# TensorE's order fixed by hand in an attention + FFN kernel: first batch by token chunk, q turned on TensorE, column-tiled v projection, q loads held back

## The chip, the cores and the metric

One core of a Trainium2 chip. The time is device microseconds of one execution, the median over several; a profiled execution gives the traces. The span in a profile runs from the first to the last instruction and is 1.7 to 3.5 us shorter than the time of the same execution. The kernel before took 481.86 us (481.56 to 485.2, three runs).

## The reference

```python
# q, k, v: 8 batches x 8 heads x 1024 tokens x 64; E, F: 64 x 1024
k_proj = einsum('ks,bhsd->bhkd', E, k)
v_proj = einsum('ks,bhsd->bhkd', F, v)
attn   = softmax(q @ k_proj.T / 8)                 # 1024 x 64 per head
x      = (attn @ v_proj), heads side by side       # 8192 x 512
h      = maximum(maximum(x @ w1, x @ w2), x @ w3)  # 8192 x 768
out    = h @ w_out                                 # 8192 x 512, fp32
```

## The kernel before

The matmuls take bf16; inputs are cast from fp32 by the load DMAs, issued from GpSimd (POOL). Each load of q, k or v brings one batch. For every batch VectorE copies q into a packed tile `q_p`, and a transpose DMA, issued from SyncE, turns it into `qT`, which the scores read.

```python
loads = ctx.enter_context(tc.tile_pool(name="loads", bufs=2))   # q_t, k_t, v_t: two of each
...
def attention(b, box):
    q_t, k_t, v_t = load(b)
    q_p = att.tile([P, NPAIR, SI, 2, D], BF16, name="q_p")
    for g in range(NPAIR):
        nc.vector.tensor_copy(out=q_p[:, g]..., in_=q_t[:, 2 * g:2 * g + 2, :, :])
    qT = att.tile([P, NPAIR * SI, P], BF16, name="qT")
    nc.sync.dma_start_transpose(out=qT, in_=q_p...)
    yield
    ...                                  # k projection (64 columns), transpose of it: kpT
    for si in range(SI):                 # v projection, fT twice side by side in lhsT
        nc.tensor.matmul(out=vp_ps, lhsT=fT2[:, si]..., rhs=v_t[:, :, si, :], ...)
    ...
    for g in range(NPAIR):               # 64x64 matmuls in groups of four (busy 0.41 us a group)
        ...                              # scores, exp
        yield
        ...                              # sums z and values av; 1/z as exp(-ln z); xT = av * zi
        yield

def ffn(b, xT):
    for ch in range(NCHUNK):             # two chunks of 512 tokens
        for jt in range(NJT):            # six steps: 12 matmuls of 128x512, then the maxout
            ...
            nc.scalar.copy(out=h1s, in_=h_ps[0])
            nc.vector.tensor_tensor(out=m12, in0=h_ps[1], in1=h1s, op=ALU.max)
            nc.vector.tensor_tensor(out=hT[:, jt, :], in0=h_ps[2], in1=m12, op=ALU.max)
            yield
        ...                              # 24 matmuls with w_out, copies, one 1 MB store
        yield
```

Attention of batch b+1 is interleaved with the FFN of batch b, one `yield` for one `yield`; the framework's scheduler then orders each engine's queue by its own estimate of when things are ready.

The softmax here doesn't subtract the row's maximum and nothing guards it: scores larger than these inputs give would overflow.

## Time and profile before

| stretch of the 475.6 us span | TensorE idle, us |
|---|---|
| 0 to 98 us | 66.6 |
| 98 to 470.3 us | 1.0 |
| 470.3 to 475.6 us (last copy and store) | 5.3 |

The idle times are stretch minus TensorE's busy time in this view of stretches (columns: stretch, its length, then busy time and count of TensorE, its weight loads, VectorE, ScalarE, POOL; granted TensorE clock, DMA share, which can read above 1, GB/s moved):

```profile
0.00:49.40 49.40, 3.69 (x34) 2.88 (x35) 4.04 (x11) 1.28 (x1) 12.02 (x20) 1.00 1.10 181
49.40:98.00 48.60, 27.71 (x146) 10.06 (x145) 15.34 (x25) 16.30 (x19) 4.38 (x5) 0.83 1.23 201
98.00:128.70 30.70, 30.66 (x161) 11.83 (x161) 16.43 (x26) 18.07 (x23) 1.76 (x2) 0.94 0.98 187
128.70:470.30 341.60, 340.68 (x1807) 144.38 (x1806) 152.18 (x217) 156.41 (x222) 7.88 (x9) 1.00 0.35 84
470.30:475.60 5.30, 0.00 (x0) 0.00 (x0) 0.00 (x0) 0.55 (x1) 0.00 (x0) 0.84 0.47 198
```

The chain of waits, in order of time (start, duration, what the end of the kernel hung on then):

```profile
14.28 35.10 DMA qT<-q_p
...
66.36 31.48 DMA qT<-q_p
97.88 0.64 PE ps_a L162 x4
...
128.74 4.35 PE ps_f L219 x19
...
144.66 1.73 PE ps_p L145 x8
...
177.90 4.35 PE ps_f L219 x19
...
470.27 0.59 ACT o_acc L226
```

Two transposes of 35.1 and 31.5 us hold up TensorE at the start. In the median a transpose takes 7.3 us from issue to landing, so these two share the DMA engines with something: the page's 40 slices show about 200 GB/s from 12 to 119 us, because loads run two batches ahead. From 98 us on TensorE is gapless, and one batch takes 177.90 - 128.74 = 49.2 us. Its v projection is eight matmuls a batch, 1.73 us in the chain; in the list of groups (busy us, mean ns of one; the first batch's eight, just after 28.9 us in which TensorE waited, took 3.54 us in the chain instead of 1.73):

```profile
L145 PE MATMUL ps_p<-v_t,fT_92 128*128 128x512 bf16 x64 | 16.8, 410 | 0.0
```

### The profile page before, as it was taken

Reading aid. Unit: us, or ns where it says so; the run is one execution under the profiler, and the core shown is the slowest. Engines: PE = TensorE matmul, PEld = TensorE weight load, DVE = VectorE, ACT = ScalarE, POOL = GpSimd, SP = SyncE. Lnnn points to the kernel's source line nnn. Section 1 sums busy time; section 2 is a strip of 40 time slices with the busy share of each in tenths; the row PEclk is TensorE's granted clock in tenths of the full one; section 3 lists DMA queues with packets and bytes.
Section 4 is the critical chain, followed back from the end, with each engine's and each line's share of the span. In section 5 each row is a group of like instructions: output and inputs, shape, how many; then the busy total and the mean of one; then the engine's idle time right before and its main releaser. Section 6 shows DMA issues by size and latency. Waiting matters only on the chain.

```text
span 475.6 us, 5314 instructions
## 1 busy us (share of the span) xinstructions
PE 402.7 (85%) x2144; PEld 169.1 (36%) x2144; DVE 188.0 (40%) x277; ACT 192.6 (41%) x265; POOL 26.0 (5%) x36
## 2 busy tenths in 40 slices
PE   0200679079999999999999999999999999999995
PEld 0100124023344434443443344434443444334442
DVE  0300156035633463435443634363435453454251
ACT  1000562036524653366236641664266415652322
POOL 7110002000010000000010001000000000000000
PEclk9999979779999999999999999999999999999999
DMA  7999999999589232944276236614101020202012
GB/s 120 202 201 196 206 206 196 196 208 216 109 176 170 97 90 88 144 123 90 88 110 156 64 114 94 150 35 121 45 10 79 0 90 0 91 0 88 34 55 88
DMA packets 62839, 54.06 MB, mean 114 GB/s; under 512 B 33760, under 2 KB 60640, under 8 KB 60768
## 3 DMA queue, kind: packets, MB, share of 16 engines
q0 software_dynamic: 27488, 28.58, 37.7%
q1 hardware_dynamic: 35328, 25.17, 18.2%
q8 instruction: 16, 0.26, 0.2%
q14 instruction: 7, 0.06, 0.0%
HBM read 57.15 MB, written 16.78 MB: 155 GB/s over the span
## 4 chain that ended last, share of the span: by engine, by line
PE 73%; DMA 18%; ACT 5%; issue 2%; DVE 1%; POOL 0%; POOLq 0%; DVEq 0%
PE ps_f L202 47%; PE ps_f L219 16%; DMA qT<-q_p 16%; PE ps_a L178 3%; PE ps_p L145 3%; PE ps_a L162 2%; DMA k_t<-in_k_dram 2%; ACT zl L185 2%; ACT zi L187 2%; PE ps_p L122 1%; ACT pT L169 1%; POOL q_t L99 0%; DVE hT L213 0%; DVE m_2011 L212 0%; DVE m_3352 L212 0%
## 5 line engine op out<-in xcount | busy, mean ns | idle before, releaser
L202 PE MATMUL ps_f<-xT,w_sb 128*128 128x512 bf16 x1152 | 265.7, 382 | 1.8 <-DVE xT L188 1.8
L202 PEld LDWEIGHTS <-w_sb 128*128 128x128 bf16 x1152 | 107.9, 98 | 142.0 <-issue 23.1
L219 PE MATMUL ps_f<-wout_sb,hT 128*128 128x512 bf16 x384 | 87.7, 379 | 0.9 <-DVE hT L213 0.3
L210 ACT COPY h1s<-ps_f 128x512 f32<-128x512 f32 x96 | 55.9, 583 | 75.8 <-PE ps_f L202 75.8
L188 DVE TENSOR_TENSOR xT<-ps_a,zi 128x1024 bf16<-128x1024 f32 x32 | 39.2, 1225 | 92.0 <-ACT zi L187 92.0
L169 ACT ACTIVATE pT<-ps_a 128x1024 bf16<-128x1024 f32 x32 | 32.8, 1024 | 83.5 <-PE ps_a L162 83.5
L226 ACT COPY o_acc<-ps_f 128x512 f32<-128x512 f32 x64 | 37.1, 584 | 50.7 <-PE ps_f L219 50.4
L219 PEld LDWEIGHTS <-hT 128*128 128x128 bf16 x384 | 36.3, 98 | 50.2 <-issue 5.4
L162 PE MATMUL ps_a<-qT,kpT 64*64 64x512 bf16 x128 | 14.0, 428 | 44.5 <-DMA qT<-q_p 43.9
L185 ACT ACTIVATE zl<-ps_a 128x1024 f32<-128x1024 f32 x32 | 32.8, 1024 | 44.0 <-PE ps_a L178 44.0
L187 ACT ACTIVATE zi<-zl 128x1024 f32<-128x1024 f32 x32 | 33.8, 1057 | 1.0
L162 PEld LDWEIGHTS <-kpT 64*64 64x64 bf16 x128 | 4.0, 105 | 58.4 <-issue 57.8
L109 DVE COPY q_p<-q_t 128x1024 bf16<-128x1024 bf16 x32 | 12.5, 442 | 28.5 <-DMA qT<-q_p 17.0
L145 PE MATMUL ps_p<-v_t,fT_92 128*128 128x512 bf16 x64 | 16.8, 410 | 0.0
L178 PE MATMUL ps_a<-pT,ones 64*64 64x512 bf16 x128 | 13.7, 417 | 3.3 <-ACT pT L169 3.3
L99 POOL DMA_DIRECT2D k_t<-in_k_dram x8 | 7.1, 894 | 144.3 <-PE ps_p L122 137.4
L152 ACT CAST vp<-ps_p 128x512 bf16<-128x512 f32 x8 | 4.7, 586 | 22.6 <-PE ps_p L145 22.6
L178 PE MATMUL ps_a<-pT,vp 64*64 64x512 bf16 x128 | 13.0, 392 | 0.1
L122 PE MATMUL ps_p<-k_t,eT_91 128*64 128x256 bf16 x128 | 9.9, 294 | 2.0 <-DMA k_t<-in_k_dram 2.0
L99 POOL DMA_DIRECT2D q_t<-in_q_dram x8 | 7.1, 888 | 65.1 <-DVE q_p L109 49.0
L99 POOL DMA_DIRECT2D v_t<-in_v_dram x8 | 7.0, 878 | 59.0 <-PE ps_p L145 54.8
L178 PEld LDWEIGHTS <-ones 64*64 64x64 bf16 x128 | 4.0, 105 | 17.2 <-issue 14.2
(219 smaller groups left out, 170.4 us busy)
## 6 DMA issues: line engine op xcount, KB each, us to landing
out_dram<-o_acc SPq DMA_DIRECT2D x16, 1024.0 KB, 3.8
q_t<-in_q_dram POOLq DMA_DIRECT2D x8, 1024.0 KB, 14.7
k_t<-in_k_dram POOLq DMA_DIRECT2D x8, 1024.0 KB, 12.5
v_t<-in_v_dram POOLq DMA_DIRECT2D x8, 1024.0 KB, 13.3
w_sb<-in_moe_w_dram POOLq DMA_DIRECT2D x3, 768.0 KB, 27.4
wout_sb<-in_moe_w_out_dram POOLq DMA_DIRECT2D x1, 768.0 KB, 35.2
e_sb<-in_E_dram POOLq DMA_DIRECT2D x1, 128.0 KB, 3.0
f_sb<-in_F_dram POOLq DMA_DIRECT2D x1, 128.0 KB, 3.0
```

The lines of the kernel that those rows point to most:

```text
L99: nc.gpsimd.dma_start(out=t, in_=src.rearrange("h (p si) d -> p h si d", si=SI))
L145: nc.tensor.matmul(out=vp_ps, lhsT=fT2[:, si].rearrange("p x k -> p (x k)"), rhs=v_t[:, :, si, :], start=(si == 0), stop=(si == SI - 1),)
L162: nc.tensor.matmul(out=sc[c * HALF:(c + 1) * HALF, hp, :], lhsT=kpT[rows, g % 2, g // 2, :], rhs=qT[rows, g * SI + 4 * c:g * SI + 4 * c + ...
L169: nc.scalar.activation(out=pT, in_=sc, func=AF.Exp, scale=scale)
L178: nc.tensor.matmul(out=dst[hp * HALF:(hp + 1) * HALF, c, :], lhsT=ones[rows] if w is None else w[rows, 2 * g + hp, :], rhs=pT[rows, hp, :] ...
L185: nc.scalar.activation(out=zl, in_=z, func=AF.Ln)
L187: nc.scalar.activation(out=zi, in_=zl, func=AF.Exp, scale=-1.0)
L188: nc.vector.tensor_tensor(out=xT[:, g].rearrange("a (c si) p -> a c (si p)", c=2), in0=av, in1=zi, op=ALU.mult,)
L202: nc.tensor.matmul(out=h_ps[i], lhsT=w_sb[i][:, ct, jt * P:(jt + 1) * P], rhs=rhs_x[:, ct, :, :], start=(ct == 0), stop=(ct == NCT - 1),)
L210: nc.scalar.copy(out=h1s, in_=h_ps[0])
L219: nc.tensor.matmul(out=o_ps, lhsT=hT[:, jt, tt * P:(tt + 1) * P], rhs=wout_sb[:, jt, :], start=(jt == 0), stop=(jt == NJT - 1),)
L226: nc.scalar.copy(out=o_acc[:, tt, :], in_=o_ps)
```

## The change

The intent: no transpose DMA in the first batch, an earlier first FFN matmul, a shorter attention on TensorE, and no transposes starved by loads. All PSUM tiles come from one pool of eight, TensorE's order is the program's order, and attention work hangs on fixed FFN steps. Core of the diff (cut, and the plan and the stores in shorthand; the softmax and FFN arithmetic is the same in halves):

```diff
-    loads = ctx.enter_context(tc.tile_pool(name="loads", bufs=2))
+    loads = ctx.enter_context(tc.tile_pool(name="loads", bufs=1))
+    psum = ctx.enter_context(tc.tile_pool(name="psum", bufs=8, space=bass.MemoryType.PSUM))
+    ctx.enter_context(tc.manual_schedule(engines={mybir.EngineType.PE}))
...
+    nc.gpsimd.dma_start(out=k_t, in_=view(k, 0))                       # k first
+    nc.gpsimd.dma_start(out=q_t[:, :, 0:SPC], in_=view(q, 0)[:, :, 0:SPC])   # then half of q
...
+    load_w(0, 1)                                                       # weights in slices
...
     def load(b):
+        dma = nc.gpsimd.dma_start(out=q_t, in_=view(q, b))
+        if b - 1 in last_T:                     # q of b waits for the transpose of b-1
+            tc.add_manual_dep(dma.ins, last_T[b - 1].ins.name, ... Sync ...)
+        nc.gpsimd.dma_start(out=k_t, in_=view(k, b))
+        nc.gpsimd.dma_start(out=v_t, in_=view(v, b))
+    def q_by_dma(b):                            # VectorE copies, then the transpose DMA
...
+    def q_by_pe(b, g, c):                       # batch 0 only: 8 transposes on TensorE
...
     for si in range(SI):                        # v projection
-        nc.tensor.matmul(out=vp_ps, lhsT=fT2[:, si]..., rhs=v_t[:, :, si, :], ...)
+        for hh in range(2):
+            nc.tensor.matmul(out=ps[hh * HALF:(hh + 1) * HALF, 0:4 * D], lhsT=fT[:, si, :],
+                             rhs=qkv[b][2][:, 4 * hh:4 * hh + 4, si, :], ...)
...
+    plan, batch 0:   (0, 2): [sc(0, 0, c1), sc(0, 1, c1), qd(1)], ...   # qd = q_by_dma
+                     (1, 1): [kv(1)], (1, 2): [kt(1), sc(1, 0), ld(2)], ...
+    plan, later b:   (0, 0): [qd(n)], (0, 2): [kv(n)], (0, 3): [kt(n), ld(n + 1)],
+                     (0, 4): [sc(n, 0)], (0, 5): [zav(n, 0), sc(n, 1)], ...      # n = b+1
+    stores of 256 tokens, the last ones of 128, instead of 512
```

## The prediction

> **What bounds the kernel now.** From about 128 us on TensorE is gapless: in the chain of waits a batch takes 49.2 us (128.74 to 177.90), of which 192 FFN matmuls at 0.216 us are 41.4 and attention 7.8. Before that DMA bounds it: in the 40 slices the queues move about 200 GB/s from 12 to 119 us (loads run ahead), and the q transpose, 7.3 us alone, shares with them and takes 35.1 and 31.5 us. In the chain these two stand before the scores; the second stall ends at 98 us. After the last FFN matmul (470.3 us) come 5.3 us of copy and 1 MB store.
>
> **What the change does.**
> 1. Batch 0: q is turned on TensorE by token chunk, without transpose DMA. k lands at about 12 us (now the first 1 MB lands at 12.5); projection and 32 cold transposes reach 18 us; then ScalarE paces (16 activations at 0.58 us, vp copies, multiplies). FFN starts at about 31 us instead of 69.
> 2. v projection column-tiled: 1.72 us becomes 0.99 (what k takes). Five groups of 64x64 matmuls instead of eight, about 0.1 us each. Batch period 48.1: 7 us in all.
> 3. Last stores per 128 tokens: tail 3.5 us.
> 4. q loads wait for the previous transpose, so transposes run at about 7.3 us.
>
> **What it costs.** The changed kernel's instruction order shows VectorE with q copies in its queue where q is not there yet. Loads come as k1, v1, q1, then q2 (after transpose 1), q3 (after transpose 2). VectorE blocks, PSUM isn't freed, TensorE stops:
> - Copies of q1 stand before the maxout of step 3 of batch 0's first chunk (about 45 us). About 9.6 MB come first; at 200 GB/s[...], q1 lands at about 55. Stall 10 us.
> - q2 lands 17 us after q1 (copies 1.9, transpose 7.3, load 8): stall 1 to 2.
> - q3 lands 17 us after q2; its first copy stands ahead of a maxout and the kT copy in step 2 of batch 0's second chunk, which the scores need: stall 12 us.
> - After each long stall TensorE restarts cold (granted clock 0.50 at 90 to 100 us now[...]): 2 us each.
> - Batch 0's second chunk: ScalarE 4.1 us per step against TensorE 3.7: 2 us.
> Later q loads are late too, but the slack of the down steps covers them.
>
> **Sum.** q1 at 55; scores of batch 1 resume 36 later (91); rest of batch 0 18; seven FFN batches and six attentions 330; cold starts, small stalls and tail 8: span 447. Runs now read 3 to 6 us above the span: 451 us, 8 in 10 between 437 and 466. Faster by over 2%: 0.93; within 2%: 0.055; slower: 0.015.
>
> **What would show it.** FFN start near 31 us; VectorE waits of about 10 us on q loads (L141) two or three times before 100 us, then little; TensorE gapless from there at a period of 48; transposes near 7 us; v projection 1.0.
>
> **What would make it wrong.** Faster loads (q1 at 48) or VectorE waits hidden by PSUM slack: 437 or less. q late in every batch, [...]: 460 and more.

What is cut: an allowance for the loads of weight slices, a second ground for the cold restarts, and two risks among those for 460 and more. The sum came to 447 us of span, 451 of time, and is left as it was, though the allowance is cut: 9.6 MB at 200 GB/s are 48 us, and the allowance is part of what was added up to q1's landing at 55. What the traces show for three other terms: "cold" is 4.33 us for 12 FFN matmuls after the second stall (98.52 us in the chain before) against 2.70 later; 0.1 us for a group of 64x64 matmuls is an estimate from the timeline before, where a group of four took 0.34 us until the next matmul (198.07 to 198.41) and one of eight 0.56 (201.10 to 201.66), 0.12 more than 0.22 for every four; 8 us for a load is assumption; in the kernel before the fastest load of k took 9.4 us from issue to landing, that of q 9.8.

## The result, and the profile after

461.56 us (458.25 to 463.42, four runs) against 481.71 (479.01 to 485.2, four runs); ratio 0.957, 95% interval 0.949 to 0.965. Ratios here are the mean time of one kernel's fast runs over that of the other's of the same rounds, so not quite the ratio of the medians.

The same view of stretches, now of the changed kernel (span 460.0 us):

```profile
0.00:28.20 28.20, 15.37 (x106) 8.42 (x106) 5.64 (x13) 10.08 (x19) 15.30 (x25) 1.00 1.24 173
28.20:48.00 19.80, 19.11 (x106) 7.43 (x105) 7.37 (x14) 7.86 (x14) 1.95 (x3) 1.00 1.31 204
48.00:56.00 8.00, 0.00 (x0) 0.00 (x0) 1.99 (x5) 0.12 (x1) 0.00 (x0) 0.69 0.79 132
56.00:79.00 23.00, 21.98 (x116) 9.49 (x115) 9.95 (x19) 8.32 (x15) 0.87 (x1) 0.89 0.68 134
79.00:94.00 15.00, 0.53 (x6) 0.25 (x6) 3.34 (x9) 0.95 (x2) 2.63 (x3) 0.59 0.99 180
94.00:136.00 42.00, 38.52 (x230) 16.31 (x226) 20.69 (x37) 21.26 (x42) 2.62 (x3) 0.94 0.89 163
136.00:338.70 202.70, 193.62 (x1101) 87.83 (x1098) 95.33 (x157) 97.17 (x185) 9.62 (x11) 0.97 0.56 117
338.70:455.90 117.20, 117.13 (x619) 51.92 (x618) 52.92 (x80) 54.09 (x102) 0.00 (x0) 1.00 0.16 56
455.90:460.00 4.10, 0.00 (x0) 0.00 (x0) 0.00 (x0) 0.56 (x1) 0.00 (x0) 1.00 0.35 130
```

| TensorE idle, us | before | after |
|---|---|---|
| start (before: to 98 us; after: to 136 us) | 66.6 | 40.5 |
| middle | 1.0 | 9.2 |
| tail | 5.3 | 4.1 |

The start has 26 us less idle time, and 8 us were given back in a stretch that had been gapless: 136 to 338.7 us holds 9.1 us without TensorE work. Its busy total rose by 3.5 us (402.7 to 406.3). 19.2 less idle and 3.5 more busy make, but for rounding, the 15.6 us by which the span fell.

Where the idle time went, in the chain of waits after:

```profile
38.05 15.94 DMA q_t<-in_q_dram
...
55.47 7.29 DMA qT<-q_p
63.32 11.39 DMA q_t<-in_q_dram
...
82.92 9.54 DMA q_t<-in_q_dram
...
107.64 5.52 DMA qT<-q_p
113.71 10.90 DMA q_t<-in_q_dram
...
153.47 5.51 DMA qT<-q_p
159.54 12.94 DMA q_t<-in_q_dram
...
338.70 5.29 PE bank L305 x24
...
375.89 0.87 PE bank L198 x16
...
385.97 5.29 PE bank L305 x24
...
455.87 0.58 ACT o_sb L312
```

The long transposes are gone (5.5 to 7.3 us each), and in their place stand loads of q, one after the other with the transposes: the rule of the diff shows as transpose, then load, then copies, then the next transpose. From batch 1 on that next transpose also waits for a free `qT` (there are two): the copies of batch 4's q were through at 127.3 us, but its transpose starts at 153.47, when the last scores of batch 2 (153.02 us) have read theirs. After the last q (275 us) batches take 385.97 - 338.70 = 47.27 us; before that they take up to 53.9 us (steps between the w_out groups that start at 136.11, 185.73, 237.58 and 291.43 us are 49.6, 51.9 and 53.9). By the list of waits VectorE stands 74.6 us, seven times, at most 12.8 us, before q copies (columns: who waits for whom; us in total, times, longest):

```profile
DVE q_p L141 <- DMA q_t<-in_q_dram: 74.6, 7, 12.8
```

How a late q stops TensorE is seen in the timeline (start, us, engine, line, instruction, and in brackets the idle time before it and what ended it):

```profile
54.01 1.43 DVE L141 COPY q_p<-q_t 128x1024 bf16<-128x1024 bf16 x4 [12.83 <-DMA q_t<-in_q_dram]
55.36 0.68 DVE L294 TENSOR_TENSOR m_436<-bank,h1s 128x512 f32<-128x512 f32 x1
...
56.09 0.64 PE L242 MATMUL bank<-pT,vp 64*64 64x512 bf16 x2 [8.61 <-DVE m_436 L294]
...
92.48 0.43 DVE L141 COPY q_p<-q_t 128x1024 bf16<-128x1024 bf16 x1 [11.02 <-DMA q_t<-in_q_dram]
...
93.42 0.28 DVE L190 COPY kpT<-bank 128x256 bf16<-128x256 bf16 x1
...
93.76 0.64 PE L225 MATMUL bank<-qT,kpT 64*64 64x512 bf16 x4 [14.14 <-DVE kpT L190]
...
172.50 1.43 DVE L141 COPY q_p<-q_t 128x1024 bf16<-128x1024 bf16 x4 [10.49 <-DMA q_t<-in_q_dram]
...
174.59 1.06 PE L172 MATMUL bank<-k_t,eT 128*64 128x256 bf16 x16 [2.29 <-DVE m_1421 L294]
```

The maxout m_436 had its data at about 44 us. It stood in VectorE's queue behind the q copies: it starts when the copies are through, at 55.36 us. Until then its bank isn't free and TensorE waits 8.6 us. The same thing happens at 92.5 us with the small copy of the k projection, which the scores need: 14.1 us. The copies stand there because VectorE's order is still the scheduler's (e4 shows that freeing TensorE's order too changes nothing in this): it moved VectorE's copies of q up to two batches earlier than the program has them. Batch 5's, for one, ran at 172.5 us in the first FFN step of batch 2 (last two lines); the program has them after the first step of batch 4. Presumably it took q to be ready there; no run shows what it assumed.

### The profile page after: what moved, and what is told of

Same layout as the page of the kernel before. It is cut to its first block, busy times and chain, and to the rows that moved or that the text cites. A ratio compares the mean times of both kernels' runs of the same rounds, so it can differ in the third digit from the quotient of the medians.

```text
span 460.0 us, 5849 instructions
## 1 busy us (share of the span) xinstructions
PE 406.3 (88%) x2272; PEld 181.7 (39%) x2272; DVE 197.2 (43%) x328; ACT 200.4 (44%) x377; POOL 33.0 (7%) x45
## 4 chain that ended last, share of the span: by engine, by line
PE 60%; DMA 29%; issue 4%; DVE 3%; ACT 2%; POOL 0%; POOLq 0%; DVEq 0%
PE bank L284 39%; DMA q_t<-in_q_dram 19%; PE bank L305 13%; DMA qT<-q_p 8%; PE bank L242 3%; DMA k_t<-in_k_dram 2%; PE bank L172 2%; PE bank L198 2%; PE bank L225 2%; DVE q_p L141 1%; ACT pT L235 1%; DVE hT L295 0%; ACT zl L256 0%; PE bank L156 0%; ACT zi L258 0%
## 5 line engine op out<-in xcount | busy, mean ns | idle before, releaser
L284 PE MATMUL bank<-xT,w_sb 128*128 128x512 bf16 x1152 | 266.1, 387 | 2.7 <-DVE m_950 L294 1.8
L292 ACT COPY h1s<-bank 128x512 f32<-128x512 f32 x96 | 56.4, 589 | 102.6 <-PE bank L284 82.1
L305 PE MATMUL bank<-wout_sb,hT 128*128 128x512 bf16 x384 | 85.8, 380 | 0.0
L235 ACT ACTIVATE pT<-bank 128x512 bf16<-128x512 f32 (+1 forms) x72 | 39.2, 598 | 48.3 <-PE bank L225 48.2
L268 DVE TENSOR_TENSOR xT<-bank,zi 128x512 bf16<-128x512 f32 x64 | 41.3, 686 | 36.3 <-ACT zi L258 35.9
L256 ACT ACTIVATE zl<-bank 128x512 f32<-128x512 f32 x64 | 35.1, 597 | 42.7 <-PE bank L242 42.1
L312 ACT COPY o_sb<-bank 128x512 f32<-128x512 f32 x64 | 36.9, 593 | 27.9 <-PE bank L305 27.9
L141 DVE COPY q_p<-q_t 128x1024 bf16<-128x1024 bf16 x28 | 10.3, 422 | 74.6 <-DMA q_t<-in_q_dram 74.6
L258 ACT ACTIVATE zi<-zl 128x512 f32<-128x512 f32 x64 | 37.1, 632 | 0.0
L225 PE MATMUL bank<-qT,kpT 64*64 64x512 bf16 x128 | 16.3, 409 | 14.6 <-DVE kpT L190 14.4
L211 ACT CAST vp<-bank 64x256 bf16<-64x256 f32 x16 | 5.8, 364 | 33.8 <-PE bank L198 19.5
L242 PE MATMUL bank<-pT,ones 64*64 64x512 bf16 x128 | 17.6, 411 | 1.8 <-ACT pT L235 1.8
L213 DVE CAST vp<-bank 64x256 bf16<-64x256 f32 x16 | 6.8, 427 | 14.1 <-ACT vp L211 13.9
## 6 DMA issues: line engine op xcount, KB each, us to landing
v_t<-in_v_dram POOLq DMA_DIRECT2D x7, 1024.0 KB, 13.5
q_t<-in_q_dram POOLq DMA_DIRECT2D x7, 1024.0 KB, 12.9
```

The costliest lines, as they stand in the source:

```text
L141: nc.vector.tensor_copy(out=q_p[:, g].rearrange("p si h d -> p h si d"), in_=qkv[b][0][:, 2 * g:2 * g + 2],)
L225: nc.tensor.matmul(out=sc[hp][c * HALF:(c + 1) * HALF, :], lhsT=kpTs[b][rows, g % 2, g // 2, :], rhs=qTs[b][rows, lo:lo + SPC, :], start=T ...
L235: nc.scalar.activation(out=pTs[b, g][r, hp, :], in_=sc[hp][r], func=AF.Exp, scale=scale)
L242: nc.tensor.matmul(out=dst[hp * HALF:(hp + 1) * HALF, :], lhsT=w(rows, hp), rhs=pTs[b, g][rows, hp, :], start=True, stop=True,)
L256: nc.scalar.activation(out=zl, in_=z[c], func=AF.Ln)
L258: nc.scalar.activation(out=zi, in_=zl, func=AF.Exp, scale=-1.0)
```

## The experiments

All kernels gave a correct result. Times are medians of four runs; each group of four experiments ran on a chip of its own, none of them beside the changed kernel, so small differences between groups should not be read. The record calls a run slow when it is over 1.5% above the fastest of its kernel. The kernel before, run beside them, scattered more than the others: 478.1 to 491.2 us in the first four experiments' rounds, 478.2 to 490.2 in the next four's (where six of seven runs lay above 486), 479.7 to 493.7 in the last four's. The comparisons with it are therefore marked unclear where a verdict was given, though most effects below are far larger than that scatter; smaller ones are read from the profiles.

My theory after reading the trace: what the change still loses is VectorE standing in order before q loads that come late; not DMA bandwidth, and not TensorE's own work. Rivals: the loads themselves are the limit; or the hand order on TensorE is what paid.

### e1_copies_held: the copies of batches 2 to 7 stay at their program place

```diff
+            cp = nc.vector.tensor_copy(out=q_p[:, g]..., in_=qkv[b][0]...)
+            if b >= 2:      # an order on VectorE's queue only: after the last maxout issued so far
+                tc.add_manual_dep(cp.ins, last_max[0].ins.name, ... NoSync, SCHED_ONLY ...)
```

> The changed kernel with one edit: VectorE's q copies of batches 2 to 7 are kept at their place in the program (after the first FFN step of the batch before), instead of one batch earlier where the scheduler put them. My theory: what the change still loses after 77 us is VectorE standing in order before q loads. From the trace: the stall of 79 to 94 us and its cold restart (18.5 us by comparison with an undisturbed second chunk), 3.8 us in batch 1, and 2.3, 4.6 and 6.6 us in batches 2 to 4, in all 36 us; so 424 to 428 us, VectorE waits for q only before batch 1's copies (about 13 us), every batch from 1 on at 47.3 us. Rival: the DMA queues are the limit and the wait only moves to the transposes and scores: 450 us or more, TensorE waiting on qT.

Measured: 428.21 us (427.25 to 429.13), span 426.8. The timeline shows the copies 47.27 us apart, with no wait before them but the first:

```profile
54.38 1.43 DVE L142 COPY q_p<-q_t 128x1024 bf16<-128x1024 bf16 x4 [13.89 <-DMA q_t<-in_q_dram]
100.77 1.42 DVE L142 COPY q_p<-q_t 128x1024 bf16<-128x1024 bf16 x4
148.04 1.42 DVE L142 COPY q_p<-q_t 128x1024 bf16<-128x1024 bf16 x4
```

The theory holds, in size too: 33 us against 36 expected (428.2 is just outside the range). The waits did not move to transposes (5.5 to 7.3 us) or scores.

### e2_q1_late: batch 1's copies later as well

```diff
-                (0, 2): [sc(0, 0, c1), sc(0, 1, c1), qd(1)],
+                (0, 2): [sc(0, 0, c1), sc(0, 1, c1)],
...
-                (0, 5): [zav(0, 2, c1), zav(0, 3, c1)],
+                (0, 5): [zav(0, 2, c1), zav(0, 3, c1), qd(1)],
```

> As the run before, and the copies of batch 1's q too are moved, from step 2 to step 5 of batch 0's first chunk. My theory: the stall of 48 to 56 us and its cold restart (about 2 us) go as well, the transpose still lands (about 63 us) before the scores of batch 1 are due (about 68): 413 to 418 us. Rival: the loads themselves bound the first 60 us (q1 can't be had sooner), the stall turns into a wait of batch 1's scores for qT or k: 424 or more.

Measured: 415.85 us (414.78 to 417.48), ratio to before 0.865 (interval 0.858 to 0.872). TensorE has almost nothing left to wait for from 30 us on (stretches as above):

```profile
0.00:30.00 30.00, 15.47 (x108) 8.50 (x109) 6.58 (x15) 10.09 (x19) 15.90 (x26) 0.88 1.24 174
30.00:90.00 60.00, 58.53 (x351) 25.34 (x350) 32.02 (x56) 34.26 (x64) 3.98 (x5) 0.97 1.00 185
90.00:410.00 320.00, 320.00 (x1814) 143.19 (x1813) 159.64 (x259) 155.79 (x293) 13.13 (x15) 1.00 0.52 114
```

q1 still landed at about 55 us; VectorE waited 3.3 us for it, and TensorE no longer at all. Loads were not the limit. This version beats both kernels.

### e3_no_throttle: the changed kernel without the rule on q loads

```diff
-        if b - 1 in last_T:
+        if False:
```

> The changed kernel without the rule that a q load waits for the transpose of the batch before (the single q buffer stays, so it waits for the copies). My theory: each q comes 7 us sooner, a transpose now shares with one load and takes 8 to 14 us; the VectorE waits shrink but stay: 445 to 456 us. Rival: the rule is what keeps transposes alive, without it they take 30 us as in the kernel before: 470 or more.

Measured: 449.88 us (449.11 to 451.1), 12 us faster than with the rule (0.937 of before, against 0.957). VectorE's wait on q loads fell from 74.6 to 22.6 us (plus 12.3 on earlier transposes), and transposes took up to 16.4 us instead of 7.3. In the changed kernel as it stands, the rule costs more than it gives.

### e4_pe_free: TensorE's order left to the scheduler

```diff
-    ctx.enter_context(tc.manual_schedule(engines={mybir.EngineType.PE}))
```

> The changed kernel with TensorE's order left to the scheduler too. My theory: the order by hand is worth little, since TensorE was gapless before from 128 us on and the gain came from the start and from smaller tiles: 455 to 468 us. Rival: the hand order is what pays: 475 or more.

Measured: 466.15 us (464.65 to 468.52), 1% above the changed kernel (not run side by side). The VectorE waits on q are the same (77.9 us, seven times). The hand order on TensorE alone is worth little here, where VectorE's waits set the time; with the copies late (e2) it was not tested.

### e5_before_pe_turn: only TensorE transposes in batch 0, in the kernel before

```diff
+        if b == 0:      # 64 small transposes through PSUM, VectorE copies
+            ...
+        else:
             ...         # q_p and the transpose DMA as before
```

> The kernel before, with one part of the change: batch 0's q is turned on TensorE (64 small transposes) instead of by a transpose DMA. My theory: the first stall (to 49 us) goes and batch 0's FFN starts near 35 us, but the transpose of batch 1 still shares the queues with loads that run ahead and takes 20 to 30 us, so only part of the first stall is gained: 456 to 470 us. Rival: the start is all there is to gain and this alone equals the whole change or better: 455 or less, no long transpose left.

Measured: 472.94 us (472.37 to 474.15); the kernel before beside it 478.2 to 490.2. Just outside my range. The mechanism held, and more came with it: the transpose of batch 1 was issued at 45 us among the loads and took 32.0 us to land (TensorE waited 7.1 us for it), that of batch 2 took 41.0 us; VectorE's next q copies waited 15.8 us for the latter, a maxout stood behind them, and TensorE waited 10.7 us. Turning q on TensorE removed one stall and left the others.

### e6_before_throttle and e7_before_both: the rule in the kernel before, alone and with e5

```diff
+            if nm == "q_t" and b - 1 in last_T:      # e6; e7 has e5's edit too
+                tc.add_manual_dep(dma.ins, last_T[b - 1].ins.name, ... Sync ...)
```

> The kernel before, with another part alone: a q load waits for the transpose of the batch before. My theory: the transpose of batch 0 still takes about 30 us (its own loads and the weights are ahead of it), that of batch 1 falls from 31 us to 15 or less, and VectorE now waits for late q loads as in the changed kernel: 455 to 472 us. Rival: no gain, the time is lost again in the q loads: 476 or more.

> Both parts in the kernel before (no hand order, no smaller tiles, no token chunks in the start). My theory: they carry most of the change's gain at the start; batch period still 49.2 us; VectorE waits for q loads: 443 to 462 us. Rival: they overlap and give no more than one alone: 463 or more.

Measured: 514.17 us (512.2 to 516.22) and 493.24 us (492.09 to 495.71). Both expectations were wrong: the rule makes the kernel before slower, by 36 us against the one fast run beside it (478.18), and still by 15 us with e5's part; the rivals' times were right. The list of waits of e6 has the changed kernel's trouble, and more of it:

```profile
DVE q_p L118 <- DMA q_t<-in_q_dram: 83.8, 7, 20.6
```

The first transpose still took 30.1 us to land, and only then was q of batch 1 loaded.

### e8_before_v_tiled: only the column-tiled v projection

```diff
+            for half in range(2):
                 nc.tensor.matmul(
-                out=vp_ps, lhsT=fT2[:, si]..., rhs=v_t[:, :, si, :],
+                    out=vp_ps[half * HALF:(half + 1) * HALF, 0:4 * D], lhsT=fT2[:, si, half, :],
+                    rhs=v_t[:, 4 * half:4 * half + 4, si, :],
```

> The kernel before, with the column-tiled v projection alone. My theory: 0.8 us per batch on a gapless TensorE, 5 to 7 us in all: 472 to 478 us, v projection 1.0 us per batch. Rival: [...] the four small copies eat the gain: 480 or more.

(Cut: a second supposed cause in the rival.)

Measured: 474.6 us (473.92 to 475.38). Against the scattered runs of the kernel before that says little, but the k loads, one a batch, come 48.5 and 48.6 us apart (188.99, 237.52, 286.14 us) instead of 49.6 and 49.3 (188.73, 238.30, 287.56): 0.6 to 1.0 us a batch, and the v projection takes 1.0 us (194.01 to 195.01), as expected.

### e9_late_no_throttle: e2 without the rule

> The version with all q copies late (e2), without the rule that a q load waits for the previous transpose. Theory now: the rule itself is no gain; it made q late, and lateness hurt only because VectorE stood before it. With the copies late there is slack: a transpose may share with one load (8 to 14 us instead of 6) and nothing waits: 413 to 419 us, as e2. Rival: transposes need the rule: 424 or more, scores waiting on qT.

Measured: 464.87 us (463.59 to 467.12), 49 us slower than e2. My theory (rule useless, lateness the only trouble) fell. The list of waits:

```profile
PE bank L233 <- DMA qT<-q_p: 36.5, 6, 8.3
```

Without the rule the load of the next q starts in the same moment in which the copies free the single q buffer, which is when the transpose starts (trace: transpose at 155.29, load at 155.53 us; behind it in the queue follow k at 159.64 and v at 160.51). The transposes then took 15.8 us in the median instead of 5.7. With the copies at their program place a transpose has about 10 us until the scores want it (in e2 184.72 to 194.97 us: FFN steps and the projections). 16 is too long: TensorE waits 6 us in each of six batches and restarts slowly (12 matmuls in 4.2 us instead of 2.7).

### e10_before_hold and e11_before_hold_throttle: held copies in the kernel before, without and with the rule

> The kernel before with one edit: VectorE's q copies of batches 1 to 7 are kept at their program place, after the first FFN step of the batch before; no rule on loads. Theory: the transpose of batch 1 starts near 72 us when most run-ahead loads are done, takes 15 us or less instead of 31, and the second stall shrinks from about 16 us to 5 or less; the first (to 49 us) stays; batch period 49.2: 462 to 474 us. Rival: the loads keep the queues full to 119 us whatever the copies do, the transpose still takes 25 us or more: 478 or more.

> The kernel before with the held copies and the rule that a q load waits for the previous transpose (which alone made it 514 us). Theory: the rule costs only through VectorE standing before a late q, so with held copies it costs nothing: as the run before within 1.5%, no VectorE wait on q loads after batch 1. Rival: the rule costs by itself, q or the transposes come too late in every batch: 490 or more.

Measured: 490.7 us (488.83 to 497.3), ratio 1.022; and 465.07 us (464.63 to 465.84), ratio 0.964. Held copies alone do not help, and e10 missed its range. Batch 1's transpose did shrink as expected (15.2 us, TensorE waited 5.2 us), but the next three took 15.7 to 16.0 us as well, which the expectation had left out: TensorE waits for transposes five times (29.4 us in the first batch, 28.9 without the edit; 19.5 in the next four). With the rule the transposes take 9.7 us in the median, and TensorE has no gap of note from about 93 us on (read in 40 slices), with a period of 49.2 us. The range for e11 itself (within 1.5% of e10) was missed by far, since e10 was not what I took it for.

Held copies and the rule together, in both kernels (us):

| | copies where the scheduler puts them | copies at their place |
|---|---|---|
| before, no rule | 481.7 | 490.7 |
| before, rule | 514.2 | 465.1 |
| changed, no rule | 449.9 | 464.9 |
| changed, rule | 461.6 | 415.9 |

("At their place" is e2 in the last row and e9 above it, batch 1's copies moved too.) The rows come from different groups of runs; the effects are larger than that scatter, but for the 9 us of the first. Each part alone does little or harm; the two together pay, in either kernel.

### e12_warm: e2 plus dummy matmuls in the idle start

```diff
+    warm(12)                 # 128x512 matmuls nobody reads, while k loads
     kp = proj_k(0)
...
+        warm(4)
         sums(0, g, (0,))
```

> The version with late copies (e2) plus 32 dummy matmuls of 128x512 on constant data in the idle start of TensorE (12 while k loads, 4 before each sum and 4 before the values of the first chunk). Theory: [...] (matmuls 0.63 us apart from 0.38 later, the first 24 FFN matmuls took 8.5 us in the changed kernel, 5.2 when warm); dummies keep it warm, 3 to 5 us less: 410 to 413 us, the first 24 FFN matmuls in 5.2 to 6 us. Rival: the start is paced by loads and ScalarE and the dummies only get in the way: 415 or more.

(The granted clock of the changed kernel reads 1.00 from 12 to 28 us. 0.63 and 0.38 us are lengths of single matmuls in its trace.)

Measured: 415.98 us (415.34 to 417.71): no gain in time. The dummies did part of what they should: projection in 1.06 us instead of 1.92, the first FFN matmul in 0.38. But the first FFN step waits for the multiplies of xT one by one (26.2 to 28.5 us), and after that its weight loads started 0.43 us apart until 31.5 us, so that the first 24 FFN matmuls still took 8.5 us (26.2 to 34.7), not 5.2 to 6; in the first 90 us VectorE waited 6.2 us for ScalarE before such multiplies, and 4.3 us for q1. The first FFN step of batch 1 comes at 84.32 instead of 85.30 us: 1 us is left, and it is lost in the scatter. That fits the rival, a start paced by loads and ScalarE.

## Why the prediction was right or wrong

The time (461.56 in a range of 437 to 466) and the direction were right. The point forecast was 10 us low, and the prediction had itself listed "q late in every batch" with "460 and more" under what would make it wrong: that case came, and the time is in the range only because the range reaches past it. Point by point:

- FFN start at 31 us: 28.2. Right.
- VectorE stops before q1, q2 and q3, and TensorE with it. Right, nearly to the microsecond: q1 copies at 54.0 us (55 predicted), q2 20.7 us later (17), q3 17.8 after that (17); TensorE stalls of 8.6 (10), about 1 (1 to 2) and 14.1 us (12). Experiments e1 and e2 show the cause.
- Cold restarts of 2 us. Right: the first 12 FFN matmuls after each long stall took 4.7 and 4.9 us instead of 2.7, at a granted clock of 0.50 (57.3 to 60 and 94.3 to 98.3 us). It had read 1.00 until 48 us, when the first stall began, and 0.88 from 48 to 52.
- Batch period 48.1 us: 47.27 in batches without a q load; v projection 0.87 us directly after the k projection. Right in kind, better by 0.8 us.
- Tail 3.5 us: 4.1. The stores gained 1.2 us, not 1.8.
- "Later q loads are late too, but the slack of the down steps covers them." **This step failed.** VectorE waited 7.7, 10.5, 11.1 and 12.1 us in batches 1 to 4. Batches 2 to 4 took 49.6, 51.9 and 53.9 us instead of 47.3: 13.5 us more; batch 1's first chunk lost about another 4. These 17 us are more than the forecast was low; the shorter period and the earlier FFN start gave part back. The mis-sized term is the load: I assumed 8 us from issue to landing, which no load of q, k or v in the trace before had reached; the last three took 12.9, 13.2 and 13.6. The slack itself was there: TensorE went on until 172.3 us after VectorE had stopped at 162.0, 10.3 us, while VectorE was held up 12.5 us (wait, copies and a maxout); with a load 5 us shorter that would be about 7.5 us (an estimate from these numbers), and nothing lost. In those stretches output stores share the DMA engines (issues at 162.6 us and after; 151 to 157 GB/s in all); that they are the cause is argued, not tested. Even the later k loads took 9.2 to 9.4 us, not 8.
- "q loads wait for the previous transpose, so transposes run at about 7.3 us" was listed as a gain. The transposes did, but e3 shows that in this kernel the rule cost 12 us net: what it gave to transposes it took from loads that VectorE stood before. e9 and e11 show the rule is needed as soon as the copies come at their place.

What stays open: what lengthened the late q loads; what the hand order is worth once VectorE no longer waits; why the kernel before scatters more than most of the others; and how the changed kernel's start would split between token chunks and load order, which no run took apart.

## What to carry to other kernels

When one engine's order is fixed by hand, look at the queues of the others: an instruction that waits for a transfer holds up what is queued behind it (here a maxout for about 11 us, and through it TensorE for 8.6), and a scheduler may put it far too early, here by up to two batches. Give each link of load, copy, transpose, use its own slack, and change them together: a rule that keeps transfers apart and a late place for the consumer each cost time alone in the changed kernel (12 and 15 us against the version with neither), and together they gained 34 (449.9 without both, 461.6 and 464.9 with one, 415.9 with both). Before crediting a change with its result, undo its parts one at a time; here the first part in the title (hand order) was worth about 1% in the kernel as it stood.

## What the traces show of transfers and idle gaps

- A transpose DMA of 1 MB took 5.5 to 5.7 us at best, 15.8 in the median with a 1 MB casting load started at the same time and two more 4 and 5 us later (e9), and 30 to 41 us among run-ahead loads (the kernel before, e5, e6).
- With weight slices among the loads (rows of 256 or 512 B as written, twice that as read) the queues moved 189 to 191 GB/s as written (20 to 28 us of the changed kernel), 8% below the 206 to 208 from 36 to 52 us. That row length is the cause was not tested.
- Loads that read 2 MB of fp32 and write 1 MB of bf16 took 9.2 to 9.4 us at best (k in the changed kernel), and the queues moved 206 to 208 GB/s from 36 to 52 us. These are bytes written (the 28.3 MB that the profile counts for the loads' queue are the size of the bf16 tiles); as read it is twice as much.
- 32 dummy matmuls in TensorE's idle start shortened the first projection from 1.92 to 1.06 us and gained 1 us of 415 (e12), where other engines and the loads set the pace.
